# Unread products next to long stretches of small products, chosen by a running sum in the planner

One core of one Trainium2 chip. The metric is the time of one execution in microseconds (us), the median of several executions; most of the argument also reads one profiled execution of each kernel. Ratios are the mean time of one kernel's fast runs over that of the other kernel's fast runs of the same rounds on the same chip, so they are not quite the ratio of the medians that are quoted. The experiments ran on different chips (the kernel before had medians from 287.2 to 291.3 us on them), so compare kernels by their ratios.

A run counts as fast here when it is at most 1.5% above the fastest run of the same kernel on that chip. Differences of about 1% are not settled here.

## The reference

Gated delta-rule attention over 32 heads, then a softplus feed-forward layer on all 3072 tokens.

```python
# q, k, v, g: 4 x 8 x 768 x 48, beta: 4 x 8 x 768
k_n = k / (norm(k) + 1e-6)
state = zeros(B, H, 48, 48)
for t in range(768):
    y[:, :, t] = g[:, :, t] * einsum('bhd,bhde->bhe', q[:, :, t], state)
    v_old = einsum('bhde,bhd->bhe', state, k_n[:, :, t])
    state += beta[:, :, t] * einsum('bhd,bhe->bhde', k_n[:, :, t], v[:, :, t] - v_old)
x = y.transpose(0, 2, 1, 3).reshape(3072, 384)
h = x @ w_in                                   # 384 x 2048
out = (maximum(h, 0) + log1p(exp(-abs(h)))) @ w_out   # 2048 x 384
```

## The kernel before

The attention is done in chunks, with many small products (16 to 64 rows, 16 to 64 columns each); the feed-forward layer gives large ones (128 rows, 256 to 512 columns), and the small and the large are mixed so that the large fill the gaps of the small. The mixing isn't written by hand. Every piece of work is an item with an engine, a fixed cost and a priority (a table of tuned numbers, `RANK`). A planner in Python places the items one after another on a model of the engines, and emits the instructions in just that order. So the plan is the kernel.

```python
class Plan:
    BLOCK = 128          # the planner's products in one block of instructions
    FETCH = 3.5          # the planner's us for a block to arrive
    WAIT = 0.168272762528
    BUSY = {"POOL": 8.5, "ACT": 2.3, "DVE": 2.5}    # an engine's first free time
    ...
    def run(self):
        ...
        while any(left.values()):
            ...                      # choose engine e, item it, start t0
            if e == "PE" and fresh is not None:      # the item starts a fresh bank
                t1 = max(free[e], since)
                k = min(40, int((t0 - t1 - 0.2) / (0.45 if t0 < 12 else 0.24)))
                if k > 0:
                    self.fill(fresh, k)              # k unread products ahead of it
            it.fn()                                  # emit the item
            ...
                it.end = free[e] = t0 + cost
            if e == "PE":
                ...
                block = issued // self.BLOCK
                issued += it.mm          # counts the item's products, not the unread ones
                ...
```

An "unread product" (a fill, below) is a product that nobody reads. It is meant to keep TensorE busy, so that the clock stays up. It is written to a bank that is free (in the traces one of the tiles d, h and o):

```python
    def fill(bank, k):
        for _ in range(k):
            nc.tensor.matmul(
                bank.ap.rearrange("p (a t) -> p a t", t=C),
                ident,
                mask[:, None, :].broadcast_to([P, 8, C]),
            )
```

`mask`, its operand, is made by GpSimd behind eight loads of `beta`. Before the change a fill is only put where the planner itself sees TensorE idle.

## Time and profile before

| | before |
|---|---|
| time, median of 3 (lowest to highest) | 286.97 us (284.70 to 287.44) |
| span of the profiled execution | 287.4 us |
| TensorE busy | 251.3 us, 87% |
| mean granted TensorE clock | 0.914 |
| fills in all / after 39 us | 103 / 16 |

The prediction shows the lines of the profile and what they say of the kernel before.

### The profile page before, as it was taken

How to read it: one execution, taken by the hardware profiler on the slowest of the kernel's cores; microseconds unless marked ns; L12 is line 12 of the kernel's file. 1: busy time of each engine (PE TensorE's matmuls, PEld its weight loads, DVE VectorE, ACT ScalarE, POOL GpSimd, SP SyncE). 2: the span in 40 equal slices, each digit the busy share in tenths (PEclk: the TensorE clock that was granted, in tenths of full speed). 3: DMA queues.
4: the chain of work that ended last, by engine and by line, in shares of the span. 5: the costliest groups of instructions: out<-in, count | busy, mean ns of one | idle time of the engine just before them, and what ended most of it. 6: DMA issues, size and time to landing. Idle time of an engine off the chain costs nothing.

```text
span 287.4 us, 14216 instructions
## 1 busy us (share of the span) xinstructions
PE 251.3 (87%) x6535; PEld 155.8 (54%) x6535; DVE 144.1 (50%) x290; ACT 140.3 (49%) x235; POOL 102.9 (36%) x182
## 2 busy tenths in 40 slices
PE   0998978894799988889999899959889999999993
PEld 0455455583556764535555455635546655667661
DVE  1599977594503774437484267545346502342110
ACT  3279365364716525637537374017845456513340
POOL 8543020842086751006899014850384000000000
PEclk9999987597569999759999799997999999999999
DMA  8999999999807999899978999995003310022112
GB/s 116 164 156 182 196 166 163 151 169 181 151 6 136 153 134 149 143 147 160 149 141 120 151 147 152 165 149 106 5 5 52 84 39 5 2 57 58 27 30 55
DMA packets 125932, 32.48 MB, mean 113 GB/s; under 512 B 119856, under 2 KB 125104, under 8 KB 125872
## 3 DMA queue, kind: packets, MB, share of 16 engines
q1 hardware_dynamic: 122752, 28.32, 63.8%
q0 software_dynamic: 3120, 3.24, 7.1%
q8 instruction: 51, 0.84, 1.3%
q14 instruction: 9, 0.07, 0.1%
HBM read 25.26 MB, written 4.72 MB: 104 GB/s over the span
## 4 chain that ended last, share of the span: by engine, by line
PE 69%; SPq 11%; DVE 7%; issue 5%; DMA 4%; ACT 1%; POOL 0%; DVEq 0%; POOLq 0%
PE h L1351 23%; PE o L1389 21%; SPq L380 11%; PE d L1069 3%; PE d L1127 2%; PE d L980 2%; PE d L935 2%; DMA qf<-in_q_dram 2%; PE d L1219 2%; PE d L1428 2%; PE d L1025 2%; PE d L1164 2%; DMA kqt<-kn 2%; PE d L578 1%; PE d L734 1%
## 5 line engine op out<-in xcount | busy, mean ns | idle before, releaser
L1372 ACT ACTIVATE ga<-h 128x512 f16<-128x512 f32 x96 | 57.2, 598 | 49.3 <-PE h L1351 47.1
L1351 PE MATMUL h<-xt,w_in 128*128 128x512 f16 (+1 forms) x384 | 80.0, 351 | 0.3 <-issue 0.3
L1389 PE MATMUL o<-w_out,ga 128*128 128x384 f16 x384 | 73.1, 336 | 1.3 <-DVE osb L1411 1.2
L1389 PEld LDWEIGHTS <-ga 128*128 128x128 f16 x384 | 36.6, 100 | 26.3 <-issue 5.1
L1351 PEld LDWEIGHTS <-w_in 128*128 128x128 f16 x384 | 36.4, 103 | 23.3 <-issue 5.5
L1411 DVE COPY osb<-o 128x384 f32<-128x384 f32 x24 | 13.3, 554 | 42.1 <-PE o L1389 42.0
L561 DVE CAST u<-d 128x384 f16<-128x384 f32 x24 | 13.4, 556 | 41.7 <-PE d L1127 23.5
L1428 PE MATMUL d<-mask,ident 128*128 128x512 f16 x103 | 28.3, 418 | 6.7 <-POOL mask L304 6.7
L495 POOL TENSOR_TENSOR ss<-ss,half_c 128x32 f32<-128x32 f32 x4 | 21.8, 5447 | 11.1 <-DVE ss L458 10.8
L845 POOL TENSOR_TENSOR tt<-tt,tmp 128x30 f32<-128x30 f32 (+7 forms) x60 | 22.7, 378 | 4.7
L838 POOL TENSOR_TENSOR tmp<-nn,tt 128x30 f32<-128x30 f32 (+7 forms) x60 | 21.8, 363 | 4.5
L827 POOL TENSOR_TENSOR nn<-ln,beta_l 128x256 f32<-128x256 f16 x8 | 4.8, 619 | 46.4 <-DVE ln L803 35.1
L1428 PEld LDWEIGHTS <-ident 128*128 128x128 f16 x103 | 10.1, 105 | 17.9 <-issue 8.5
L539 POOL CAST qn<-qf 128x768 f16<-128x768 f32 x12 | 10.1, 844 | 26.0 <-DMA qf<-in_q_dram 22.6
L559 ACT CAST u<-d 128x384 f16<-128x384 f32 x24 | 11.5, 479 | 14.4 <-PE d L1127 7.3
L1113 DVE TENSOR_TENSOR w<-vf,d 128x384 f16<-128x384 f32 x22 | 11.2, 546 | 11.7 <-PE d L1069 10.5
L754 ACT ACTIVATE kk<-d 128x256 f16<-128x256 f32 x24 | 8.2, 383 | 17.2 <-PE d L738 13.4
L773 DVE TENSOR_TENSOR mt<-d,mask 128x256 f16<-128x256 f32 x24 | 9.0, 417 | 13.5 <-ACT kk L754 7.6
L451 ACT ACTIVATE ksq<-kf 128x768 f32<-128x768 f32 x12 | 10.1, 842 | 10.3 <-DVE osb L1411 4.8
L803 DVE STREAM_TRANSPOSE ln<-kk 128x1024 f16<-128x1024 f16 x6 | 11.4, 1903 | 7.0 <-ACT kk L754 4.3
L1286 DVE TENSOR_TENSOR yg<-d,gf 128x384 f16<-128x384 f32 x24 | 12.2, 547 | 5.0 <-PE d L1219 3.4
L559 ACT COPY kqt<-d 128x1024 f16<-128x1024 f16 (+1 forms) x12 | 11.3, 952 | 6.0 <-PE d L578 5.9
(84 smaller groups left out, 327.9 us busy)
## 6 DMA issues: line engine op xcount, KB each, us to landing
kf<-in_k_dram SPq DMA_DIRECT2D x24, 192.0 KB, 5.3
qf<-in_q_dram SPq DMA_DIRECT2D x24, 192.0 KB, 5.4
vf<-in_v_dram SPq DMA_DIRECT2D x24, 192.0 KB, 5.3
gf<-in_g_dram SPq DMA_DIRECT2D x24, 192.0 KB, 5.5
out_dram<-osb SPq DMA_DIRECT2D x48, 96.0 KB, 3.0
w_in<-in_moe_w_in_dram POOLq DMA_DIRECT2D x2, 768.0 KB, 9.2
w_out<-in_moe_w_out_dram POOLq DMA_DIRECT2D x1, 1536.0 KB, 15.3
beta_l<-in_beta_dram POOLq DMA_DIRECT2D x8, 12.0 KB, 4.3
```

What stands on the lines that cost most here:

```text
L380: nc.sync.dma_start(out=b.ap[64 * b2 : 64 * b2 + 64].rearrange("t p h d -> t (p h) d"), in_=x[2 * b2 : 2 * b2 + 2, :, t0 : t0 + C].rearran ...
L495: lambda ss=ss, r=r: nc.gpsimd.tensor_tensor(ss.ap[:, r], ss.ap[:, r], half_c[:, r], ALU.pow),
L559: nc.scalar.copy(d, x)
L561: nc.vector.tensor_copy(d, x)
L838: eng.tensor_tensor(t, nn.ap[:, :, j + 1 :, j : j + 1].broadcast_to([P, 2, n, w]), tt.ap[:, :, j : j + 1, 16 : 16 + w].broadcast_to([P, 2, ...
L845: eng.tensor_tensor(rows, rows, t, ALU.add)
L1286: lambda m=m, yg=yg, yp=yp, gf=gf: nc.vector.tensor_tensor(heads(yg.ap, m), hd(yp[m].ap), heads(gf.ap, m), ALU.mult),
L1351: nc.tensor.matmul(hp.ap[:, n * b : n * b + n].rearrange("p (a t) -> p a t", t=P), w_in[:, j, f * P : (f + 1) * P], xt.ap[:, t0 // P : (t0 ...
L1372: lambda hp=hp, o=gb: nc.scalar.activation(o.ap, hp.ap, AF.Softplus),
L1389: nc.tensor.matmul(op.ap[:, :DM], b.ap[:, c + c0 : c + c0 + 128], w_out[:, f, :], start=(f == 0), stop=(f == NF - 1),)
L1411: lambda op=op, ob=ob: nc.vector.tensor_copy(ob.ap, op.ap[:, :DM]),
L1428: nc.tensor.matmul(bank.ap.rearrange("p (a t) -> p a t", t=C), ident, mask[:, None, :].broadcast_to([P, 8, C]),)
```

## The change

The intent: the planner shall also put fills where TensorE is busy, but with small products, so that the clock doesn't fall there (in before it goes to half at 50.55 and at 122.23 us, after windows of 3.41 us with 219 and 132 products). A running sum of the planned TensorE work of the last 3.4 us (small products counted at 0.6) is kept; below 1.8 us up to three fills are added. The planner's time then moves on by their length (`t0 += extra`). Besides, the mask is made ahead of the loads of `beta`, and TensorE's first free time is 4.5 us.

```diff
-    BUSY = {"POOL": 8.5, "ACT": 2.3, "DVE": 2.5}
+    BUSY = {"POOL": 8.5, "ACT": 2.3, "DVE": 2.5, "PE": 4.5}
...
+        done = []
...
+            extra = 0.0
             if e == "PE" and fresh is not None:
                 t1 = max(free[e], since)
                 k = min(40, int((t0 - t1 - 0.2) / (0.45 if t0 < 12 else 0.24)))
+                work = sum(
+                    w * max(0.0, min(b, t0) - max(a, t0 - 3.4)) for a, b, w in done[-40:]
+                )
+                if t0 > 20 and work + 0.21 * max(0, k) < 1.8:
+                    more = min(3, int((1.9 - work) / 0.21) - max(0, k))
+                    k = max(0, k) + more
+                    extra = 0.21 * more
                 if k > 0:
                     self.fill(fresh, k)
+                    done.append((t0 - 0.21 * k, t0, 1.0))
+            if e == "PE":
+                t0 += extra
+                done.append((t0, t0 + it.cost, 1.0 if it.mode == "full" else 0.6))
             it.fn()
...  (the eight loads of beta_l, unchanged, are moved from ahead of the mask to behind it)
```

`RANK` is unchanged.

More of the change, by code (lines that the diff above doesn't have):

```diff
@@ L286 @@
     nc.vector.tensor_copy(ident, ident32)
+    mask = consts.tile([P, C], F16, name="mask")
+    nc.gpsimd.memset(mask, 1.0)
+    for r in range(2):
+        nc.gpsimd.affine_select(
+            out=mask[64 * r : 64 * r + 64],
+            in_=mask[64 * r : 64 * r + 64],
+            compare_op=ALU.is_ge,
+            fill=0.0,
+            base=-1,
+            pattern=[[1, C]],
+            channel_multiplier=-1,
+        )
     beta_l = consts.tile([P, NSS, HC], F32, name="beta_l")
@@ L299 @@
                 )
-    mask = consts.tile([P, C], F16, name="mask")
-    nc.gpsimd.memset(mask, 1.0)
-    for r in range(2):
-        nc.gpsimd.affine_select(
-            out=mask[64 * r : 64 * r + 64],
-            in_=mask[64 * r : 64 * r + 64],
-            compare_op=ALU.is_ge,
-            fill=0.0,
-            base=-1,
-            pattern=[[1, C]],
-            channel_multiplier=-1,
-        )
     w_in = consts.tile([P, 3, FF], F16, name="w_in")
```

## The prediction

> **What bounds the kernel now.** I read the page first: the busy shares, the clock row and the DMA row, then the chain that ended last.
>
> ```profile
> PE 251.3 (87%) x6535; PEld 155.8 (54%) x6535; DVE 144.1 (50%) x290; ACT 140.3 (49%) x235; POOL 102.9 (36%) x182
> PEclk9999987597569999759999799997999999999999
> DMA  8999999999807999899978999995003310022112
> q8 instruction: 51, 0.84, 1.3%
> PE 69%; SPq 11%; DVE 7%; issue 5%; DMA 4%; ACT 1%; POOL 0%; DVEq 0%; POOLq 0%
> ```
>
> TensorE is busy for 87% of the span and holds 69% of the chain, and its clock falls in several places between slices 6 and 28. The DMA engines are near full until about 200 us. In order of time the chain is loads alone until TensorE takes over at 40.66 us:
>
> ```profile
> 33.94 5.69 DMA qf<-in_q_dram
> 39.78 0.84 POOL qn L539
> 40.66 1.05 PE d L578 x8
> ```
>
> So what TensorE does before 40 us is not on the path; after it the chain is mostly TensorE, in program order, with few waits for data. Next the windows view, with stretches cut where the clock changes (us, length, PE busy, PEld, DVE, ACT, POOL, clock, DMA share, GB/s):
>
> ```profile
> 47.14:50.55 3.41, 2.85 (x219) 2.41 (x218) 2.44 (x5) 1.32 (x4) 0.94 (x1) 1.00 1.02 160
> 50.55:57.38 6.83, 5.42 (x174) 3.33 (x164) 3.67 (x11) 1.99 (x5) 5.72 (x2) 0.50 0.98 153
> 64.20:67.62 3.42, 0.53 (x62) 0.48 (x49) 3.42 (x7) 2.43 (x4) 1.74 (x3) 1.00 1.27 186
> 67.62:84.68 17.06, 14.60 (x344) 9.32 (x347) 4.12 (x7) 6.10 (x8) 5.22 (x13) 0.50 0.65 109
> 118.82:122.23 3.41, 2.40 (x132) 1.85 (x131) 1.18 (x3) 2.71 (x6) 0.00 (x0) 1.00 0.85 163
> 122.23:129.06 6.83, 5.49 (x106) 2.61 (x107) 1.98 (x5) 2.66 (x6) 0.00 (x0) 0.50 0.90 146
> 190.49:193.91 3.42, 0.26 (x16) 0.26 (x16) 1.11 (x3) 0.00 (x0) 0.78 (x3) 1.00 1.11 141
> 193.91:197.32 3.41, 3.41 (x46) 1.25 (x38) 2.43 (x4) 1.44 (x4) 0.00 (x0) 0.50 0.89 170
> ```
>
> Half clock holds from 40.31 to 47.14, 50.55 to 57.38, 67.62 to 84.68, 115.40 to 118.82, 122.23 to 129.06, 159.78 to 163.19 and 193.91 to 197.32: 47.8 us, always in whole steps of 3.41 us, and after 197.32 never until the end. Two kinds of windows precede a fall: nearly empty ones (64.20, 190.49) and ones full of small products. [...] the seven windows before a fall have 0.07 to 0.41 of full streaming, every window that kept its clock has 0.44 or more, and the clock came back only after windows with 0.84 or more. Three extra products of 128x512 add 3 x 0.213 / 3.41 = 0.19, so they can lift five of the seven (0.29 to 0.41), not the two empty ones.
>
> Then I asked the timeline what ended TensorE's idle time:
>
> ```profile
> 113.13 0.22 PE L980 MATMUL d<-td,xs 32*16 32x16 f16 x9
> 114.73 0.55 PE L980 MATMUL d<-td,xs 32*16 32x16 f16 x55 [1.38 <-issue]
> 68.53 1.01 PE L578 MATMUL d<-ident,kn 128*128 128x128 f16 x8 [3.80 <-DVE mt L694]
> ```
>
> A stop of 1.38 us in the middle of 64 equal products cannot be data. Counting products from the first, this stop, those at 52.13, 78.45, 101.89, 123.58 and 158.85 and the one of 3.80 us inside the eight transposes at 68.53 all come at the same place modulo 128. They are waits for the next block of instructions; the name DVE beside 68.53 only came last.
>
> [...]
>
> **The change part by part.**
> The order of the changed kernel's instructions can be compared without running it. Unread products go from 103 to 124. The first group falls from 22 to 12 (the planner lets TensorE start at 4.5 us); from 39 us on they go from 16 to 47. And since each extra one moves the planner's time, all later work is in another order, on every engine.
>
> (1) Start. Now the first unread product waits 6.7 us for the mask, whose two instructions stand behind eight loads of beta (5.92 us on POOL). 22 of them last until 13.04 us, while the first normalised keys are ready at 10.74. In the changed kernel the mask should be ready near 2.3 us and 12 products end near 7 us, so the first transposes start near 10.8 instead of 12.87. That is 2 us earlier, but the load that lands at 39.63 sets the next step: 0 us.
>
> (2) Extra unread products: 31 after 39 us, 31 x 0.213 = +6.6 us where nothing else was waited for.
>
> (3) What they and the new order save. I cut both orders into blocks of 128 products and gave each kind its start-to-start distance in warm stretches of the trace (512 columns 0.217 us, 384 columns 0.163, the 64 of L980 0.75 us, and so on). From 39.07 to 282.61 the kernel before took 243.5 us, of which 196.4 are such dense work; the surplus is 47.1 us. Warm short blocks still take 3.3 to 3.8 us (85.00 to 88.28, 199.63 to 203.01), so a block cannot go faster than the fetch, and an unread product in a short block costs nothing. By stretch, surplus before, then my estimate for the new order with a floor of 3.45 us per block and about 0.2 us for each seam:
> - 39.07 to 61.80: 9.4 -> 7.2. The fall at 40.31 stays (no product is added ahead of it); the one at 50.55 goes, since 3 + 3 + 1 + 2 now stand about there.
> - 61.80 to 85.00: 11.1 -> 7.4. The late fetch stays (the 1.5 MB of w_out are loaded then), but 12 more MoE products and both transposes stand ahead of it, so the window is not empty; a block that is almost only L935 (1.3 us dense) follows and may still lose the clock, which I count half.
> - 85.00 to 109.96: 3.3 -> 3.4.
> - 109.96 to 130.74: 8.2 -> 4.7; nine unread products ahead of L935 and groups of eight L1389 between the small ones should keep the clock.
> - 130.74 to 190.27: 5.5 -> 5.3.
> - 190.27 to 199.63: 5.1 -> 3.0; the wait for kqt should shorten, as two stores no longer stand ahead of that transpose in SyncE's queue.
> - to the end: 4.6 -> 6.8, since the new order has more short blocks here (2.1 and 2.7 us dense).
> Sum 47.1 -> 37.8, a saving of 9.3 us.
>
> Together 0 + 6.6 - 9.3 = -2.7 us: 287.0 - 2.7 = 284.3; I put 284.5.
>
> **The rivals.**
> (a) *The clock was the loss.* The dense work done in half-clock windows cost about 16 us more than warm (16 products of L1389 at 79.3 took 5.23 instead of 2.6 us). If nearly all windows stay warm and the fills hide in fetch waits, 287 - 16 + 6 + 1 = 278. For it: five of seven falls are within 0.19 of the limit. Against: after 197 us nothing can be won, and the falls at 40.31 and around 68 have causes that stay.
> (b) *The new order is the loss.* The ranks were tuned for the old order; a new wait for data or for a bank in TensorE's queue costs 1 to 4 us each, as at 190.49. With fills at full price and half of the saving: 287 + 6.6 - 4.6 = 289; with one bad wait 291.
> (c) *Loads hide it.* DMA is near full until 200 us; a TensorE that gets ahead before that waits for q, k and their transposes. Against: SyncE's queue stood still from 76 to 85 us for a store's source, so there is slack. If true, only the end counts: 287 to 288.
>
> **Range and chances.** The three runs before spread over 2.7 us[...]. 284.5, with 279.5 to 290.0 from (a) halved and (b) halved. Faster by over 2% means below 281.2, which needs most of (a): 0.22. Slower needs above 292.7, more than (b): 0.12. Within 2%: 0.66.
>
> **What would show it.** First unread product near 2.3 us, first transposes near 10.8, TensorE taking over again at 39 to 41 us; half clock near 40 as before but 20 to 35 us in all instead of 47.8; unread products from 39 us on busy for about 13 us instead of 6.3; stops still 128 products apart; the wait near 190 below 2.5 us. It is wrong if the half-clock time stays above 40 us, if a new wait for data over 3 us stands on TensorE, or if the loads end as late as before, with TensorE idle before them.

The weights in the prediction and below count a product as its columns at 0.213 us per 512, times its rows / 128, as a share of the window of 3.41 us. They are a yardstick of mine; that the clock counts so is not shown. The 0.213 us is an estimate, half of the 0.427 us at which fills follow one another at half clock in before's trace; at full clock they start 0.216 us apart.

## The result

| | before | after |
|---|---|---|
| time, median of 4 (lowest to highest) | 287.21 us (284.70 to 288.59) | 297.70 us (297.48 to 302.71) |
| ratio of fast runs, 95% interval | | 1.0373 (1.0283 to 1.0463) |
| span of the profiled execution (both fast) | 287.4 us | 295.8 us |
| mean granted clock | 0.914 | 0.908 |
| half clock after 39 us | 47.8 us | 47.8 us |

Slower by 3.7%, where 0.9% faster was predicted. From the page of the changed kernel, the lines that answer to the first ones of the prediction (busy time of each engine; granted clock and DMA in tenths over 40 slices; the chain that ended last by engine):

```profile
PE 257.4 (87%) x6556; PEld 158.2 (53%) x6556; DVE 145.4 (49%) x290; ACT 139.6 (47%) x235; POOL 102.8 (35%) x182
PEclk9689978687599999779985799999999899999999
DMA  8999999999919899987799899671021420022112
PE 69%; SPq 11%; issue 7%; DMA 6%; DVE 3%; ACT 2%; POOL 0%; DVEq 0%; POOLq 0%; ACTq 0%
```

TensorE is busy for 6 us longer and the clock isn't higher. In the chain, "issue", time in which TensorE waits for nothing that the profile shows, goes from 5% to 7% of a longer span. Its start in order of time (start, length, what):

```profile
34.49 5.75 DMA qf<-in_q_dram
40.39 0.84 POOL qn L553
41.27 1.04 PE d L592 x8
```

The handover from loads to TensorE is at 41.27 us instead of 40.66: as the prediction said, the start is hidden.

The fills after 39 us, from the groups by line of that stretch, first of before, then of after (count, busy us, mean ns of one). The 37 are those written to ring d; the other ten of the 47 stand with other banks:

```profile
L1428 PE MATMUL d<-mask,ident 128*128 128x512 f16 x16 | 6.3, 526 | 0.0
```

```profile
L1442 PE MATMUL d<-mask,ident 128*128 128x512 f16 x37 | 13.6, 489 | 0.2 <-DVE yg L1300 0.2
```

Now the windows of the changed kernel, cut at its clock changes (us, length, PE busy, PEld, DVE, ACT, POOL, clock, DMA share, GB/s):

```profile
60.64:70.88 10.24, 8.20 (x285) 6.82 (x284) 8.20 (x21) 8.06 (x12) 2.98 (x4) 1.00 1.28 188
70.88:81.12 10.24, 6.82 (x220) 4.09 (x210) 0.61 (x2) 3.59 (x6) 0.83 (x1) 0.50 1.07 163
122.08:128.91 6.83, 3.83 (x66) 1.63 (x69) 1.14 (x2) 0.99 (x3) 0.00 (x0) 0.50 0.88 120
149.39:152.80 3.41, 2.58 (x147) 1.82 (x150) 1.77 (x3) 3.41 (x4) 3.41 (x1) 1.00 0.88 163
152.80:166.45 13.65, 13.04 (x335) 6.61 (x337) 5.55 (x11) 3.89 (x7) 6.55 (x5) 0.50 0.99 146
227.89:231.30 3.41, 3.41 (x98) 1.54 (x86) 1.02 (x2) 0.00 (x0) 0.00 (x0) 0.50 0.91 102
```

The long half-clock stretch at 67.62 to 84.68 of before is shorter (70.88 to 81.12), and the one at 115 is gone. In their place stand one of 13.65 us from 152.80, where the kernel before had one of 3.41 us, and one at 227.89, where it was at full clock. With those at 40.16 and 53.81, which are not shown, the sum is the same to the tenth. The timeline shows how the long one begins, though six fills stand there (start, length, line, tiles, count, and idle time before it):

```profile
148.40 1.03 PE L1442 MATMUL d<-mask,ident 128*128 128x512 f16 x4
150.25 1.32 PE L949 MATMUL d<-tn,kk 16*32 16x16 f16 x128 [0.83 <-ACT tn L899]
151.51 0.60 PE L1442 MATMUL o<-mask,ident 128*128 128x512 f16 x2
```

The four fills fall mostly into the window that ends at 149.39, which was over 0.9 full anyway. In the next one stand 128 products of 16 rows, an idle gap of 0.83 us, and two fills: weighted as in the prediction, 0.35 of full streaming. The clock falls at 152.80 and comes back only after a window of more than 0.8; the three half-clock windows from 152.80 had 0.7 to 0.8. (At half clock a product takes twice as long, 0.427 instead of 0.216 us from fill to fill in before's trace, so it counts double here, as it does in the prediction's "0.84 or more".)

And the stops at the block boundaries. One of them, and the two longest rows of each kernel in the view of what TensorE waited for (total us, times, longest; from 39 us on; first before, then after):

```profile
120.72 0.30 PE L752 MATMUL d<-kqt 48*32 48x64 f16 x16
125.08 2.29 PE L1365 MATMUL h<-xt,w_in 128*128 128x512 f16 x5 [4.07 <-issue]
```

```profile
PE d L578 <- DVE mt L694: 3.8, 1, 3.8
PE d L734 <- DMA kqt<-kn: 3.2, 1, 3.2
```

```profile
PE h L1365 <- issue: 4.1, 1, 4.1
PE d L635 <- issue: 3.4, 1, 3.4
```

The wait of 3.8 us is the stop that the prediction showed at 68.53. Ahead of the stop of 4.07 us stand 128 small products, which are done in 1.9 us (119.16 to 121.02), while the packets of q8 (below) start 5.2 us apart there (116.81 and 122.03), and TensorE goes on 1.5 us after the second has ended. The wait of 3.2 us for kqt (at 190 us in before) is down to 0.7 us, below the 2.5 us that were predicted.

That the stops wait for instructions can be seen in the traces themselves, from the packets of queue q8, which the page calls instruction (51 packets, 0.84 MB, in before and in after). Each of the 23 stops of over half a microsecond in before and after ends 1.3 to 1.7 us after a packet of q8 has ended (1.1 to 2.2 us in all twenty traces); for the other waits of that length the packet lies 0.6 to 6.5 us back. And although a packet takes only 0.9 to 1.7 us, none starts sooner than 3.27 us after the one before it.

To compare many kernels I cut each trace in the same way, from the first of the small products with the triangular blocks (about 39 to 41 us) to the last product. That stretch is the sum of: 192.9 us of real products at their dense, warm distances (the same for all, from the prediction's working); fills at the estimated 0.213 us; TensorE's idle time at block boundaries ("stops"); its other idle time; and a rest, which holds what half clock adds and the seams between kinds. TensorE's queue also holds a few semaphore instructions, which take places in a block: two of them move the boundary by one product. Before has three after 39 us, and its stops move from place 95 to place 94 of 128 after the second; after has one. They are counted here. (The expectations below were written with a count that left them out. It gave 13.6 us of stops for before, and too little for every kernel with several of them.) All in us, one execution of each kernel, profiles of fast runs only:

| kernel | stretch | fills | stops | other idle | rest | half clock in it |
|---|---|---|---|---|---|---|
| before | 243.5 | 3.4 | 15.7 | 6.6 | 24.9 | 47.8 |
| after | 251.3 | 10.0 | 19.2 | 5.7 | 23.5 | 47.8 |

So of the 7.8 us in this stretch, +6.6 are fills at their full price, +3.5 stops, -0.9 other idle time, -1.4 the rest. The other half microsecond of the 8.3 by which the spans differ (before rounding) is the start.

### The profile page after: what moved, and what is told of

It reads as the page before. It is cut to its first block, busy times and chain, and to the rows that moved or that the text cites.

```text
span 295.8 us, 14267 instructions
## 1 busy us (share of the span) xinstructions
PE 257.4 (87%) x6556; PEld 158.2 (53%) x6556; DVE 145.4 (49%) x290; ACT 139.6 (47%) x235; POOL 102.8 (35%) x182
## 4 chain that ended last, share of the span: by engine, by line
PE 69%; SPq 11%; issue 7%; DMA 6%; DVE 3%; ACT 2%; POOL 0%; DVEq 0%; POOLq 0%; ACTq 0%
PE h L1365 22%; PE o L1403 21%; SPq L394 11%; PE d L1442 3%; PE d L1083 3%; PE d L1141 2%; DMA kqt<-kn 2%; PE d L949 2%; DMA qf<-in_q_dram 2%; PE d L1178 2%; DMA kf<-in_k_dram 2%; PE d L994 2%; PE d L1039 2%; PE d L1233 2%; PE d L1223 1%
## 5 line engine op out<-in xcount | busy, mean ns | idle before, releaser
L1365 PE MATMUL h<-xt,w_in 128*128 128x512 f16 (+1 forms) x384 | 75.4, 339 | 4.3 <-issue 4.1
L1442 PE MATMUL d<-mask,ident 128*128 128x512 f16 x114 | 35.3, 448 | 2.3 <-POOL mask L305 2.1
L852 POOL TENSOR_TENSOR tmp<-nn,tt 128x30 f32<-128x30 f32 (+7 forms) x60 | 22.8, 380 | 4.5
L1442 PEld LDWEIGHTS <-ident 128*128 128x128 f16 x124 | 12.4, 110 | 16.5 <-issue 7.1
L1127 DVE TENSOR_TENSOR w<-vf,d 128x384 f16<-128x384 f32 x22 | 11.2, 543 | 10.6 <-PE d L1083 8.5
L472 DVE TENSOR_REDUCE ss<-ksq 128x16 f32<-128x768 f32 x12 | 11.4, 948 | 6.0 <-ACT ksq L465 5.9
```

What stands on the lines that cost most here:

```text
L852: eng.tensor_tensor(t, nn.ap[:, :, j + 1 :, j : j + 1].broadcast_to([P, 2, n, w]), tt.ap[:, :, j : j + 1, 16 : 16 + w].broadcast_to([P, 2, ...
L1365: nc.tensor.matmul(hp.ap[:, n * b : n * b + n].rearrange("p (a t) -> p a t", t=P), w_in[:, j, f * P : (f + 1) * P], xt.ap[:, t0 // P : (t0 ...
L1442: nc.tensor.matmul(bank.ap.rearrange("p (a t) -> p a t", t=C), ident, mask[:, None, :].broadcast_to([P, 8, C]),)
```

## The experiments

The theories at the start: the fills themselves are paid and useless (theory *fills*); the new order that `t0 += extra` brings is the loss (theory *order*); the moved mask and start are (theory *start*). A fourth came up on the way: the places at which the instruction blocks end (theory *places*). The quoted expectations name theories by letters of their own; in those of e12 to e17, A is *places*, B is *order*, and C is that any disturbance is a new draw.

### The parts of the change alone: e1, e2, e3

e1_order_only takes the changed kernel and leaves the fills that the running sum adds out, but moves the planner's time as if they were there:

```diff
+                    if k > 0:
+                        self.fill(fresh, k)      # only those of the old rule
                     k = max(0, k) + more
                     extra = 0.21 * more
-                if k > 0:
-                    self.fill(fresh, k)
+                elif k > 0:
+                    self.fill(fresh, k)
```

> The order of the changed kernel with 28 of its extra unread products left out (the planner still counts their time, so every other instruction stands where the changed kernel has it); from 39 us on 19 unread products stay, against 47 in the changed kernel and 16 before. Theory A, the new order is the loss: 295 us or more, near the changed kernel's 297.7. Theory B, the unread products are the loss (28 x 0.213 = 6.0 us on the path, no half-clock time saved): 291 to 292. Theory C, the products do keep the clock up and are worth more than they cost: slower than the changed kernel, over 298.

Measured: 297.43 us, ratio 1.0219 (1.0096 to 1.0342); its profile fell on a slow run, so I read none of its waits.

e2_fills_only does the reverse: the running sum chooses fills, the planner's time stays, so the order is exactly that of before, with 27 instead of 16 fills after 39 us:

```diff
                     k = max(0, k) + more
-                    extra = 0.21 * more
...
-                t0 += extra
```

(with the mask and `BUSY` of before).

> The order of the kernel before, with the running sum choosing unread products but without moving the planner's time: 27 after 39 us instead of 16. Theory A (order): 285 to 287.5, the products stand next to fetch waits and two falls of the clock (near 50 us) go. Theory B (products): 11 x 0.213 = 2.3 us slower, 289 to 290.

Measured: 294.35 us, ratio 1.0154 (1.0055 to 1.0253). The stretch is 248.6 us, its half-clock time 41.0 us instead of 47.8. Only 2.4 of the 5.1 us more are the fills; the stops grew by 5.5 us, from 15.7 to 21.2, though no real product changed its place in the order.

e3_start_only has only the moved mask and `"PE": 4.5`.

> Only the first part of the change: the mask ahead of the beta loads, TensorE from 4.5 us in the planner, so 12 instead of 22 unread products first. Order of all else unchanged. Expected by every theory that takes the load landing near 39.6 us as the limit: within 1 us of before, first transposes near 10.8 us. If the start were on the path: 2 us faster; if the early fall of the clock (9.4 to 16.3 us in the changed kernel) mattered: 1 to 3 us slower.

Measured: 289.90 us, ratio 1.0027 (0.9991 to 1.0062). Theory *start* is out: no part of it is on the path. Order and fills each cost without the other.

### Fills where the clock really falls: e4

In the order of before, 47 fills (45 of them in the stretch of the table) were added by hand ahead of the real products at which the trace of before showed the clock falling or staying down.

```diff
+    MORE = {500: 2, 598: 3, 838: 3, 906: 2, 1214: 7, 1534: 3, 2468: 1, 2536: 3,
+            2743: 3, 2777: 3, 3660: 3, 3694: 2, 4476: 12}
...
+                k = max(0, k) + self.MORE.get(issued, 0)
```

> The order of the kernel before, and 47 more unread products put by hand into the windows after which its clock fell, each ahead of a fetch wait or of a data wait seen in its trace. If the clock is worth what I read (some 16 us of work at half speed, most of it after windows that three products lift) and products ahead of a wait are free: 277 to 281, half-clock time after 39 us under 20 us. If products cost their time wherever they stand (47 x 0.213 = 10 us) and buy no clock: 294 to 297. If the windows' phase differs from run to run, between the two and widely spread.

Measured: 296.40 us, ratio 1.0276 (1.0193 to 1.0359). The page's row of the granted clock:

```profile
PEclk9999997897759799799999999999799999999998
```

The clock did what was wanted: half-clock time 30.7 us instead of 47.8, mean clock 0.942 to 0.950 in its fast runs. The time didn't. Fills +9.6 us, stops +1.5, other idle -3.4, rest -3.8: 17.1 us less at half clock gave back little more than a fifth of that in the rest. Perhaps TensorE at a higher clock reached the next boundary or the next wait sooner and stood there; its idle time fell by only 1.9 us in spite of 45 more fills, but no run shows that this is the reason. That is the failure of the change's own aim, even where the fills are well placed.

### Again, and the order alone a second time: e5, e6

The same kernels as the result and e1.

> The changed kernel itself, beside the next one on one chip. Its ratio to the kernel before was 1.037 on another chip: 1.03 to 1.045 here. Against the order-only kernel of the same call: if the 28 left-out products are paid and buy nothing, 5 to 6 us slower than it; if they buy back half-clock time worth what they cost, within 2 us.

> The changed kernel's order without 28 of its unread products, again. If the order alone loses: ratio 1.02 or more to the kernel before. If the first result came from slow runs: 1.00 to 1.01.

Measured: the changed kernel 298.64 us, ratio 1.0385 (1.0276 to 1.0494); the order alone 295.10 us, ratio 1.0305 (1.0237 to 1.0372), so its two draws lie 0.9% apart. In e6 the fills cost 4.0 us, and its stops are 20.8 us against 15.7.

### The price of a fill, and fills taken away: e7, e8

e7_no_late is the kernel before without its own 16 late fills; e8_tail30 puts 30 fills more into the last part, where the clock of before is full (1.00 from 197.32 us to its last product).

```diff
-                if k > 0:
+                if k > 0 and issued < 600:       # e7
```

```diff
+    MORE = {n: 3 for n in (6003, 6022, 6032, 6252, 6296, 6312, 6344, 6360, 6376, 6392)}
+                k = max(0, k) + self.MORE.get(issued, 0)    # e8
```

> The kernel before without its own 16 unread products after 39 us; order unchanged. If such products are worth their time: slower, 1 to 3 us, with more half-clock time. If they cost 0.213 us each and hide nowhere: 3 us faster, ratio 0.99. If they stand in waits: the same within 1 us.

> The kernel before with 30 unread products added where the clock is always full and TensorE never waits (after 245 us), three at each of ten products of the first layer. Price of one such product: 30 x 0.213 = 6.4 us slower, ratio 1.022. If they were hidden beside weight loads or evictions: under 1.01.

Measured: e7 287.45 us, ratio 1.0044 (1.0002 to 1.0086); e8 294.29 us, ratio 1.0245 (1.0145 to 1.0344), of which the trace (of a slow run) shows the 30 as one group without an idle moment before it:

```profile
L1430 PE MATMUL h<-mask,ident 128*128 128x512 f16 x30 | 8.1, 379 | 0.0
```

0.0245 x 287 = 7.0 us for 30, so 0.23 us each; at 0.213 it would be 6.4, and the interval holds both. Fills in a dense place are paid in full. The 16 that before has are worth about what they cost, to half a per cent.

### The new order without any late fills: e9

The changed kernel with all fills from product 600 on left out. Against e7 it differs in the order (and in the start, which e3 showed to be neutral).

```diff
                 if k > 0:
-                    self.fill(fresh, k)
+                    if issued < 600:
+                        self.fill(fresh, k)
```

(in effect; the running sum and `t0 += extra` go on as in the changed kernel.)

> The changed kernel's order with no unread product at all after 39 us (the start as in the changed kernel). Beside the kernel before without its own 16 (ratio 1.004) this is the order alone. If the order itself is the loss: 1.025 or more. If the order is neutral and the products make the loss: 1.00 to 1.01.

Measured: 296.18 us, ratio 1.0280 (1.0206 to 1.0354), with no late fill at all. This is the cleanest pair of profiles, e7 against e9, both fast. The first rows of what TensorE waited for, e7 first:

```profile
PE d L980 <- issue: 3.5, 4, 1.6
PE d L935 <- ACT tn L885: 2.7, 2, 2.5
PE h L1351 <- issue: 2.7, 1, 2.7
PE d L1127 <- issue: 2.7, 4, 1.2
```

```profile
PE d L995 <- issue: 4.7, 3, 2.2
PE d L950 <- ACT tn L900: 4.4, 2, 2.6
PE d L1084 <- issue: 3.9, 2, 2.3
PE d L642 <- issue: 2.8, 1, 2.8
```

| kernel | stretch | fills | stops | other idle | rest | half clock in it |
|---|---|---|---|---|---|---|
| e7_no_late | 240.5 | 0 | 15.6 | 8.4 | 23.6 | 47.8 |
| e9_order_bare | 249.4 | 0 | 22.8 | 9.6 | 24.1 | 58.0 |
| after | 251.3 | 10.0 | 19.2 | 5.7 | 23.5 | 47.8 |

From e7 to e9 the stretch grows by 8.9 us: stops +7.2, other idle time +1.2, rest +0.5. (The spans differ by 7.0 us, since e9's stretch starts 1.9 us earlier.) Two of the stops in the timeline of e9, in the middle of equal small products:

```profile
67.28 0.36 PE L950 MATMUL d<-tn,kk 16*32 16x16 f16 x32
69.44 0.91 PE L950 MATMUL d<-tn,kk 16*32 16x16 f16 x96 [1.80 <-issue]
70.29 0.64 PE L636 MATMUL d<-kqt 48*64 48x64 f16 x32
73.72 0.41 PE L642 MATMUL d<-kqt 48*32 48x32 f16 x32 [2.79 <-issue]
```

From one stop's end at 69.44 to the next one's at 73.72 are 4.3 us, for 128 products that keep TensorE busy for some 1.5 us. In the new order such blocks are more frequent. An estimate from the traces, with each product at its warm distance, has three blocks of under 2 us in e7 and six in e9; summed over all blocks, what is missing to 3.45 us is 14 us in e7 and 22 us in e9, and the stops grew by about as much. From e9 to the changed kernel the fills then cost 10.0 us and take away 3.6 us of stops, 3.9 of other idle time and 0.6 of the rest (10.2 us less at half clock): a loss of 1.9 us in the end. So in these profiles the fills buy back most of their price, and only undo what the new order made worse.

### Other re-orderings: e10, e11

Is it this order, or any other than the tuned one? In the kernel before the planner's time is moved on once, by 0.42 us at product 1042 (e10) or by 0.21 us at product 2404 (e11); no fill is added by it on purpose.

```diff
+            if e == "PE" and issued == 1042:     # e11: issued == 2404, t0 += 0.21
+                t0 += 0.42
```

> The kernel before with one number changed in the planner: TensorE's time moved by 0.42 us at one place near 57 us, no unread product added (10 instead of 16 after 39 us). From there on 37% of TensorE's instructions stand elsewhere. If the old order is a tuned one that any shift spoils: 1.01 to 1.03. If the changed kernel's order is an unlucky one: 0.99 to 1.01.

> The same with 0.21 us at one place near 109 us; three unread products more; order differs from 112 us on. If any shift spoils the tuned order: 1.005 to 1.02; if not: within 0.5% of before.

Measured: e10 298.90 us, ratio 1.0361 (1.0283 to 1.0438); e11 300.69 us, ratio 1.0405 (1.0300 to 1.0511). A single nudge of 0.2 us, with the priorities kept, costs as much as the whole change. In e11 the loss is mostly stops, 25.2 us against 15.7. They stand at place 94 and then 93, because four semaphore instructions lie in the stretch. Other idle time is 4.3 us against 6.6, the rest 2.3 us more, half clock 54.6 us. The estimate by short blocks says only 4 us for it, so that count isn't the whole of it. e10's profile fell on a slow run and isn't read.

### Moving the block boundaries only: e12 to e15

Theory *places*: the loss comes from where the boundaries fall against the dense stretches of small products. To move them without touching order, waits or columns streamed, the one group of 29 early fills (hidden, ahead of 39 us) was split into more, smaller products.

```diff
     def fill(bank, k):
+        a, k = (2, 116) if k == 29 else (8, k)      # e12: (3, 77)
         for _ in range(k):
             nc.tensor.matmul(
-                bank.ap.rearrange("p (a t) -> p a t", t=C),
+                bank.ap[:, : C * a].rearrange("p (a t) -> p a t", t=C),
                 ident,
-                mask[:, None, :].broadcast_to([P, 8, C]),
+                mask[:, None, :].broadcast_to([P, a, C]),
             )
```

e12 and e13 do it to the kernel before, e14 to e4, e15 to e2.

> The kernel before, same order and same unread products, but the 29 unread products of 512 columns that lie ahead of 39 us (hidden, while TensorE waits for the first inputs) are issued as 77 of 192 columns: the same columns within half a per cent, 48 instructions more. Theory A (the loss of every re-ordered plan comes from where the 128-product blocks of the instruction fetch fall against the dense stretches of small products; the tuned plan sits at a good place): the stops of TensorE at every 128th product grow from 13.6 us to some 20 to 24 us, and the kernel is 4 to 9 us slower, ratio 1.015 to 1.03. Theory B (the order itself, its waits and the clock make the loss): no change, ratio 0.99 to 1.01, with stops within 3 us of those of before.

> As the last one, with the 29 issued as 116 of 128 columns: 87 instructions more, so the block boundaries move by 87 places, which is 41 places back from the old ones. Theory A: stops of some 18 to 22 us, 3 to 7 us slower, ratio 1.01 to 1.025. Theory B: ratio 0.99 to 1.01.

> The order of before with the 47 late unread products put by hand where the clock fell (e4, ratio 1.0276, stops of 17.2 us), and the same split of the 29 early ones, 87 instructions more. Theory A: a count of the work between block boundaries says that for this sequence the shift is a good one (the shortfall of the blocks is about a third less than unshifted): stops of 9 to 13 us, 4 to 8 us faster than e4, ratio 1.00 to 1.015. Theory B: as e4, ratio 1.02 to 1.035.

> The order of before with the unread products chosen by the running sum (e2, ratio 1.0154, stops of 15.9 us), and the same split. Theory A: the count of work between boundaries says a fifth less shortfall: stops of 11 to 14 us, 2 to 5 us faster than e2, ratio 1.00 to 1.01. Theory B: as e2, ratio 1.01 to 1.025.

| run | median us | ratio (95%) | unshifted | stretch | stops | half clock |
|---|---|---|---|---|---|---|
| e12_shift48 | 291.83 | 1.0166 (1.0096 to 1.0236) | before | 244.9 | 24.3 | 41.0 |
| e13_shift87 | 290.81 | 1.0081 (1.0039 to 1.0122) | before | 243.1 | 17.7 | 44.4 |
| e14_aimed_shift87 | 290.16 | 1.0138 (1.0050 to 1.0226) | e4, 1.0276 | 244.8 | 15.6 | 30.7 |
| e15_fills_shift87 | 290.42 | 1.0030 (0.9982 to 1.0077) | e2, 1.0154 | (slow profile) | | |

By the ratios alone theory *places* looked right in three of four (e13 just missed its range). The profiles say otherwise. In e12 the stops grew by 8.6 us, as the theory wanted, but the stretch only by 1.4, since other idle time fell by 3.2 and the rest by 4.0, with less half clock. In e13 the stops grew by 2.0 us and the stretch not at all, and its profiled run is 2.2 us longer because the stretch began at 41.7 us instead of 39.1: the split had cost at the start. So a control was needed.

### The control, and two uses: e16, e17, e18

e16_split128 splits the 29 into 157, so that all later boundaries fall on the same products as in the kernel before. e17 is the changed kernel with the split of e13. e18 is e2 with a shift of 90 made by splitting earlier groups.

```diff
+        sizes = [2] * 75 + [1] * 82 if k == 29 else [8] * k     # e16, in units of 64 columns
+        sizes = [2] * 4 * k if k in (22, 8) else [8] * k        # e18
```

> A control for e12 and e13: the kernel before with the 29 early unread products of 512 columns issued as 157 of 128 or 64 columns (the same columns in all), 128 instructions more, so that every block boundary after them falls on the same product as in the kernel before. Theory A (the place of the fetch blocks makes the loss of e12): from 39 us on as before, stops of 12 to 16 us and half-clock time of 44 to 51 us; what is lost is only the later start that the split itself may bring (1 to 2.5 us in the traces of e12 and e13), ratio 1.00 to 1.01, below e12 (1.0166). Rival (the split itself costs, wherever the boundaries fall): as e12 or above, ratio 1.015 to 1.025.

> The changed kernel with the same split as e13 to e15 (29 early unread products as 116, boundaries moved by 87 places). My count of the work between boundaries says the changed order has no good place: its shortfall is 19.7 us unshifted and 24.6 us shifted, so on theory A it is slower than the changed kernel (ratio 1.03 to 1.04) by some 1 to 4 us, ratio 1.04 to 1.055. Rival C (every place is a new draw of stops and clock windows, and the count says little): anything between 1.015 and 1.05, as e14 and e15 moved by 1.2 to 1.4 per cent.

> A candidate to beat both kernels: the kernel of e2 and e15 (order of before, unread products chosen by the running sum, 27 late ones), boundaries moved by 90 places as in e15, but by splitting two earlier groups (22 into 88 and 8 into 32 products of 128 columns) at a place where TensorE waits for inputs longer, so that the start at 39 to 41 us is not delayed. If e15's later start (its first small u-product at 41.1 us against 39.2 in the kernel before) was the split's doing, this gives 1 to 2 us back: ratio 0.993 to 1.001. If the place of boundaries mattered less than the rounds showed: ratio 1.00 to 1.015.

| run | median us | ratio (95%) | stretch | stops | other idle | half clock |
|---|---|---|---|---|---|---|
| e16_split128 | 296.50 | 1.0227 (1.0171 to 1.0283) | 246.7 | 20.8 | 7.0 | 41.0 |
| e17_after_shift87 | 301.40 | 1.0396 (1.0328 to 1.0464) | 255.1 | 23.2 | 4.2 | 51.2 |
| e18_fills_early_shift | 295.52 | 1.0170 (1.0108 to 1.0232) | 245.1 | 20.7 | 4.6 | 34.1 |

The control speaks against *places* as the whole cause. With every boundary on its old product, e16 is 2.3% slower, more than e12 and e13, whose boundaries moved. Its profiled run is 7.4 us longer. Of those, 4.0 come from a later start, which the timeline shows; before first, then e16:

```profile
28.48 6.43 PE L1428 MATMUL d<-mask,ident 128*128 128x512 f16 x29
39.03 0.26 PE L1025 MATMUL d<-td,kk 32*32 32x32 f16 x8 [0.54 <-issue]
```

```profile
28.92 3.52 PE L1429 MATMUL d<-mask,ident 128*128 128x128 f16 x60
34.24 3.39 PE L1429 MATMUL d<-mask,ident 128*128 128x128 f16 x97 [1.79 <-issue]
43.07 0.26 PE L1025 MATMUL d<-td,kk 32*32 32x32 f16 x8 [1.60 <-issue]
```

The 128 products more are one more block (52 packets of q8 instead of 51), and its arrival (1.79 us inside the split fills) and the next one's (1.60 us) come between loads and main stretch, so what was hidden no longer is. The other 3.2 us come from the stretch itself, where the same products in the same order at the same places in their blocks stop for 20.8 instead of 15.7 us, with 6.8 us less at half clock. That the two go together is plausible, since a TensorE that is warm has worked off its block sooner and waits longer for the next; no run takes them apart. e18, against 1.003 of e15 with nearly the same shift (90 for 87) and the same 27 late fills, is at 1.017, its start at 43.9 us. So the count of the work between boundaries says something of the stops: they rose in e12, e13 and e17 (23.2 us against the changed kernel's 19.2) and fell from e4 to e14 (17.2 to 15.6), each time in the direction that was foretold. It doesn't say the time: it foretold three of four ratios, and these were right by luck, since start, other waits and clock moved too. Each of these runs is, as it looks, a new draw of start, stops and clock windows. e17 lies inside what I had written for such draws, and just below the range for *places*.

No version was faster than the kernel before beyond the noise. By the ratios, of all 18, e3, e7, e13 and e15 are within 1% of it; every other one is slower by more, and none is faster.

## Why the prediction was wrong

By its own steps:

- **Start, 0 us: right.** The first fill stands at 2.13 us, the first transposes at 10.47, the handover at 41.27, and e3 gives 1.0027.
- **Fills, +6.6 us: right.** The late fills stream for 10.0 instead of 3.4 us, and e8 shows the price of about 0.21 to 0.23 us each where nothing else was waited for. Dense fills at full clock start 0.216 us apart in before's trace.
- **What they and the new order save, -9.3 us: wrong, and the step that failed.** The surplus over dense work went from 47.2 to 48.4 us instead of to 37.8. By the prediction's own stretches, cut at the same blocks of the queue and named by the times of the kernel before (before, predicted, measured): up to 61.8 us 9.4, 7.2, 10.0; to 85.0 us 11.1, 7.4, 7.8; to 110 us 3.3, 3.4, 5.3; to 130.7 us 8.2, 4.7, 7.7; to 190 us 5.5, 5.3, 11.1; around 190 us 5.1, 3.0, -0.1; to the end 4.6, 6.8, 6.7. Two of the seven were met within half a microsecond (the stretch to 85 us and the end), and of the loss around 190 us nothing is left, which is better than predicted. The large miss is 130.7 to 190 us, where I had entered no new fall of the clock: there it was lost from 152.80 to 166.45, 13.65 us instead of 3.41. What the runs show in place of the saving: the new order alone costs 2.2 to 3.1% (e1, e6, e9), in the profiles mostly as stops (+7.2 us from e7 to e9), and the fills, at 10.0 us, take only 8.1 us of stops, other waits and rest away again.
- **"20 to 35 us" of half clock instead of 47.8: wrong, 47.8.** I had taken each fall as a thing that three fills can lift, and none as new. What I didn't see is that the sum which decides where fills go has little to do with what the trace shows ahead of a fall. Printed while the kernel is built, it reads 2.5 to 2.65 us of 3.4 for the products that fell into the window 118.67 to 122.08. Weighted by rows in the trace that window has 0.30 of full streaming, 1.0 us, and no fill. A small product of 16 rows counts 0.6 in the planner and 16/128 = 0.13 in my weighting of the trace. And the planner's time runs ahead: it has those products at 106 us and the chip at 120. So fills came where the planner sees a lull, as at 148.40, in a window that was full. The border itself is less sharp than the prediction has it. With each product spread over its record in the trace, before's falls have 0.06 to 0.43, and in other traces a window with 0.48 fell (e3) and one with 0.38 kept its clock (e13).
- **Rival (b), "the new order is the loss": the right one, and too small.** I put it at 289 to 291 us. The order alone, without late fills, is 2.8% slower (e9), and the profile pair e7 and e9 puts most of it on stops: +7.2 us of +8.9. I had reckoned with one bad wait for data. My estimate did give every block a floor of 3.45 us, and still came out 10.6 us too low over all: it had no term for a clock that falls at a new place, and it took the new order as neutral apart from its seams and short blocks. All three new orders that ran (this one, and those of e10 and e11) cost 2.2 to 4.1%.
- **Rival (a), "the clock was the loss": refuted as far as 17 us go.** e4 took 17.1 us of half clock away and came out 2.8% slower. e14, with a mean clock of 0.959 in its fast runs against 0.937 of before on the same chip, is no faster either (1.0138; 1.001 by the medians of all runs).
- **Rival (c), "loads hide it": refuted.** TensorE's waits that a DMA ended sum to 3.2 us after 39 us in before and to 0.7 us in after.

Why a tuned plan loses by almost any nudge is argued, not shown: constants such as `WAIT = 0.168272762528` and the ranks look like the result of a search on times, which picks an order that happens to have few stops and falls in the right places; any other order with the same rules is then an ordinary draw. The kernels fit that, with ratios from 1.003 to 1.041 and none below 1. What stays open is what makes each draw what it is. Stops, clock windows, start and waits changed together in these runs, and moving only one of them was not possible: the splits also moved the start.

## What to carry to other kernels

Before adding filler work for a clock, measure with it placed by hand where the trace shows the falls: here 17 us less at half clock were worth less than the 9.6 us of fills. Keep a change of contents apart from a change of order (here, one line that moves the planner's time), since with a searched schedule a re-ordering alone cost 2 to 4%, more than what was to be won. And give every shifting experiment a control that shifts nothing: three of four expected ratios came true here, though the control, which shifts nothing, was slower than both shifted versions of the same kernel.

## What the traces show of the blocks and of the clock

- Stops at block boundaries: with streams of small products single stops of TensorE reach 4.07 us (after, at 125.08), and in the profiles of fast runs they sum to 15.6 (e7) to 25.2 us (e11). They come 128 products apart; q8 has 51 packets for before's 6535 recorded products and 52 for e16's 6663; and the stops move by one product for two semaphore instructions. No two packets of q8 start less than 3.27 us apart, and TensorE goes on 1.1 to 2.2 us after one has ended.
- Small products and the clock: in before's trace the windows ahead of a fall had 0.07 to 0.41 of full streaming when each product is weighted by its rows / 128, and those that kept the clock 0.44 or more. In after's the falls from 39 us on had 0.28 to 0.38, and 0.7 to 0.8 did not bring a half clock back. The border isn't sharp (0.48 in a fall of e3, 0.38 kept in e13). TensorE was busy for 2.58 of 3.41 us in the window from 149.39, and it fell all the same.
- What half clock costs: in e4, 17.1 us less of it changed the time that I could put to it (the rest in the table) by 3.8 us; where the other part went is open.
- Here the kernel's own fills moved the instruction blocks: e16 shows one more block ahead of the main stretch as a start 4.0 us later.
